# A gated FNet layer in split float32: y's sums placed behind the operands, part two's rows and first tokens loaded a chunk sooner, y's last copies set between the pairs of weights

## The chip, the core and the metric

One core of a Trainium2 chip runs the whole program. Its engines work at the same time, each through its own list in order: TensorE (PE) multiplies, VectorE (DVE) and ScalarE (ACT) work on elements, SyncE (SP) issues most of the DMAs, and GpSimd (POOL) does next to nothing here. An instruction waits for the results it needs, and everything behind it in the same list waits with it. The metric is the time of one execution on the device in microseconds (us).

## What is computed

S = 2048 tokens, D = 512, F = 1792, all float32:

```python
xn = layernorm(x)                                   # rows of 512
a, b = xn @ dft_hid_re.T, xn @ dft_hid_im.T
y = dft_seq_re @ a - dft_seq_im @ b                 # FNet mixing, 2048 x 512
h = relu(xn @ w1 + b1) ** 2
out = x + y * silu(h @ w2 + b2)
```

The kernel transforms along the sequence first and along the hidden dimension second; the sum is the same.

## The kernel before

**Arithmetic.** Every float32 operand is split into a high part (ACT, `split_hi`, line 77) and a low part (DVE, `split_lo`, line 80), and a product is three matmuls: high by high, high by low, low by high. Large products use a scheme of seven block products in place of eight. It needs sums of blocks of the operands, made by DVE ahead of the split (`sums_b`, lines 212 to 214: one row of 512 elements, two of 256), and sums of the seven results (`combine`, lines 255 to 265).

**Part one, first transform.** The sequence transform goes in eight chunks `c` of 256 frequencies; each goes through eight steps `j` over the tokens. Chunks 0 and 1 are plain products. Chunks 2 to 7 use the seven products: 42 matmuls in step (c, j), called group (c, j) here, line 453, on the PSUM banks m_bb, m_b and m_ba. The operand of a step is a tile of the transform's matrix: loaded by SP into `r` (two buffers, so a load waits until the split of two steps earlier has read it), summed into `t` (`prep_sums`), split into `g` (`prep_parts`). It is made two steps ahead of its use.

**Part one, second transform.** The result of chunk c - 1 (tile `plain` or `c` in the profile) is transformed along the hidden dimension while chunk c runs, again as seven products of 12 matmuls each, one per step (line 428, `y<-...`). In order of time they take the operands A11, S2, S3, A22, A12, S1, S4. `y_make(b, i)` makes operand number i: a split (`y_A`, `y_S`), and at some steps a sum of blocks (`y_sum`, line 385). `y_product` multiplies, `y_result` copies a product out or adds it (line 442, `ysb<-y,ysb`). The sixth product, S1's, begins in the same PSUM tile that the fifth one's add reads, so PE waits there for that add. Three of the seven need a sum of blocks of the hidden transform's matrix (`yw`, tiles `y_t`). `y_sums`, advanced step by step by `next(t3)`, makes these sums once, during chunk 2: it loads blocks (`y_t<-in_wd`), adds (lines 349, 353, 359, 366), splits (lines 339/340 or 77/80), and stores them to DRAM (`td`). The later chunks load them back (`y_load`, line 328), in the same two buffers.

**Weights of part two.** While chunks 3 to 6 run, `make_w` makes the sums and splits of one piece of w1 per chunk and stores it (`jobs`, `w0hi`, `w1d`).

**Part two** goes through 28 hidden units (four chunks of 512 tokens by seven pieces of F), 42 matmuls each (line 779, `hps`), on two sets of PSUM banks by turns: even units on b2, ba and bb, odd ones on b3 and bc. ACT copies a unit's first product out (line 784), DVE combines it (lines 256 to 265), ACT squares it, and it is stored (`hd`). A unit can begin only when the unit two before it is combined. Its tokens are loaded raw (`in_xt`), normalised by DVE with `rows`, the means and factors of LayerNorm (line 479, two instructions), summed and split into `xT` (`xt_half`, a generator of four steps). The tokens of the first 512 are made in chunk 7 (tile `stage`), each half in four calls of `next(staged[q])`. After the hidden units come the products with w2 (line 833).

**The passage between the parts.** y of the last chunk is not done in seven products: after the first hidden unit, `stage2` multiplies it as two plain products (line 307, `yps`), in banks bc and ba, and ACT copies each out (line 313, `ysb<-yps`). Beside it the last pieces of w1 (5 and 6, `v5`, `v6`) and two pieces of w2 (2 and 3, `w2`, `w3`; tiles `w2raw`, `w2g0a`, `w2g1a`) are loaded, summed, split and, for w2, stored; `go("w2", ...)` takes one step of each name. Both w2 pieces use the same raw buffer.

The order on every engine is that of the program: nothing is moved by a scheduler.

Of the kernel before, what the change touches and what calls it, by code (L numbers as in the profile page):

```python
# [11 lines left out]
ALU = mybir.AluOpType  # L12

P = 128
# [4 lines left out]
NC = S // CW  # L19
# [22 lines left out]
S1 = A21  # L42
# [28 lines left out]
def fnet_gated_kernel(ctx, tc, x, xt, ct, wd, w1, w2, b1, b2, out):  # L71
# [31 lines left out]
    def buf(tag, shape, name, dtype=F32, bufs=1):  # L103
        return pool.tile(shape, dtype, tag=tag, bufs=bufs, name=name)

    def bcast(src, n):
        return bass.AP(tensor=src.tensor, offset=src.offset, ap=[[0, P], [1, n]])
# [218 lines left out]
    def y_load(n):  # L326
        for q, t in enumerate(y_matrix(n)):
            nc.sync.dma_start(t.bitcast(F32), TD[n][q])
# [54 lines left out]
    def y_sum(b, to, x_, y_, op, place):  # L383
        v = y2[b]
        nc.vector.tensor_tensor(v[place], v[x_], v[y_], op=op)
        v[to] = v[place]

    def y_make(b, i):

        if i == 0:  # L390
            y_part(b, "A11", 0)
            y_sum(b, "S1", "A21", "A22", ALU.add, "A21")
        elif i == 1:
            y_sum(b, "S2", "S1", "A11", ALU.subtract, "A11")
            y_part(b, "S2", 1)
        elif i == 2:
            y_part(b, "A22", 0)

            y_sum(b, "S3", "A22", "S2", ALU.subtract, "A22")
        elif i == 3:  # L400
            y_part(b, "S3", 1)
            y_sum(b, "S4", "A12", "S2", ALU.subtract, "A11")
        elif i == 4:
            y_part(b, "A12", 1)
        elif i == 5:
            y_part(b, "S1", 0)
        elif i == 6:
            y_part(b, "S4", 1)
# [51 lines left out]
    def load_rows(c, t):  # L460

        flat = rows.rearrange("a b -> (a b)")
        for m in range(2):
            for h in range(2):
                n = m * S + c * TC + h * 256
                nc.sync.dma_start(t[:, 2 * m + 1 - h], bcast(flat[n:n + 256], 256))
        xT["rows"] = t
# [49 lines left out]
    def stores():  # L517
        while later:
            later.pop(0)()
# [44 lines left out]
    def prep_sums(between=None):  # L564
        if todo:
            s = todo[0]
            making_[s] = moving(f"{s[0]}_{s[1]}", raw[s], between)
            next(making_[s])
# [121 lines left out]
    last_plain((2, 0), (3, 0))  # L690
    split_s1(NJ - 1)
    prep(close_plain)
    next(t3)
    y_begin(1, copy.rearrange("p k (m t n) -> p k m t n", m=2, t=2)[:, :, ::-1], (0, 1, 2, 3))


# [186 lines left out]
        nc.vector.tensor_tensor(z, z, fin[c][2 + k // 2][:, k % 2, w], op=ALU.add)  # L883
        nc.sync.dma_start(at(out[c * TC:(c + 1) * TC], k)[:, cols], z.rearrange("p (k e) -> p k e", e=256))

    jobs, staged, w1_late = {}, {}, {}
    for c, j in steps:
        last = c == NC - 1
        if j == 0:
            ms = banks(c)  # L890
        g = part.pop((c, j))
        for p in ORDER:
            a, (grp, b) = PRODUCTS[p]
            mm(product(ms, p), XC[j][:, a], lambda b_: g[grp][:, b_, b], j == 0, j == NJ - 1)

        i = j - 2 + last
        done = (c - 2, 6) if j == 0 and c > PLAIN else (c - 1, i) if 0 <= i < 7 else None
        stores()
        prep_sums()

        y_make(c - 1, i + 1)
        if c == PLAIN and j in (0, 1, 4, 5, 6, 7):
            next(t3)
        if c in JOBS and j < 6:
            if j == 0:
                jobs[c] = make_w(*work.pop(0), *(buf(f"pq1{k}", [P, 4, 256], f"w{c}_{k}") for k in range(2)))
            next(jobs[c])
        if last:
            for q, js in ((0, (3, 4, 5)), (1, (4, 5, 6))):
                if j in js:  # L910
                    next(staged[q])
        if done:
            y_product(*done)
        if j == NJ - 1:
            e = buf("e", [P, 4, 512], f"c{c}")
            combine(e, ms)
            rows_ = y_result(*done)
            if not last:

                y_begin(c, e.rearrange("p (m i) (d t n) -> p (i d) m t n", m=2, d=2, t=2), (2, 3, 0, 1))  # L920
        prep_parts()
        if done:
            if j < NJ - 1:
                rows_ = y_result(*done)
            later.extend(lambda v=v: y_put(*v) for v in rows_)
        if c > PLAIN and i in (-1, 1, 3):
            y_load({-1: 2, 1: 4, 3: 1}[i])
        if c == PLAIN and j == 4:
            nc.vector.transpose(stats_t, stats.rearrange("p m h j -> p (m h j)"))
            for q in range(4):  # L930
                nc.sync.dma_start(rows[:, q * 32:(q + 1) * 32], stats_t[q * 32:(q + 1) * 32, :])
        if last:

            if j in (2, 3):
                q = j - 2
                t = buf(f"xc{2 + q}", [P, 3, 4, 256], f"stage{q}")
                if q == 0:
                    load_rows(0, t[:, 0])
                    b2s = buf("st", [P, D], "b2s")
                    nc.sync.dma_start(b2s, bcast(b2, D))  # L940
                staged[q] = xt_half(0, q, lambda k, t=t: t[:, 1 if k == "r" else 2])
                next(staged[q])
            if j == 4:
                nc.sync.dma_start(WD[0][:, :, :, CW:].bitcast(F32), B12D)
            if j > 3:
                load_w1(j - 4)
            if j == 6:
                w1_late[5] = late_w1(5)
                next(w1_late[5])
# [10 lines left out]
    def go(*names):  # L960


        for v in names:
            k, n = v[0], int(v[1:])
            if k == "m":
                load_rows(n, buf("pq00", [P, 4, 256], f"rows{n}"))
            elif k == "l":
                load_w2(n)
            elif k != "h" or n < len(units):
                if v not in making:  # L970
                    making[v] = {"h": lambda: operand(n, *units[n]), "x": lambda: tokens(n // 2, n % 2),
                                 "w": lambda: late_w2(n), "v": lambda: late_w1(n)}[k]()
                next(making[v])
# [38 lines left out]
    for n, (c, p) in enumerate(units):  # L1012
        ahead, behind = beside.get((c, p), ((), ()))
        go(*ahead)
        unit = hidden(n, c, p)
        next(unit)
        if n == len(units) - 1:

            m26, m4 = bank("b2", "m_b2_o0"), bank("ba", "m_ba_o0")
            bias(m26[:, 0], 2)  # L1020
            bias(m4[:, 0], 4)
        if before:
            next(before)
        next(unit)
        if n == 0:

            making["v5"] = w1_late[5]
            load_w1(4)
            go("w2", "v5", "v5", "v6", "w2", "w2", "w2", "w3", "v6", "v6", "w3", "w3", "w3")
            stage2(NC - 1, 0)  # L1030
            stage2(NC - 1, 1, "ba")
        go(*behind)
        before = unit
    m1, m7, m53 = bank("bb", "m_bb_o0"), bank("bc", "m_bc_o0"), bank("b3", "m_b3_o0")
    bias(m53[:, 0], 5)
# [147 lines left out]
```

## Time and profile before

| | |
|---|---|
| median of 3 runs | 752.03 us (749.72 to 752.36) |
| the profiled execution | 752.59 us, of which the span is 750.8 us |
| mean granted clock of TensorE in it | 0.973 |
| moved by DMA | 157.91 MB, mean 210 GB/s |

The profile is of one execution. Durations and waits below come from it; "idle before" is the time an engine stood ahead of an instruction, with the engine or DMA that ended the wait. The granted clock is that of the throttle on TensorE: 1.00 in most stretches of 10 us, 0.72 between 160 and 170 us, and 0.59 between 460 and 470 us.

### The profile page before, as it was taken

What the parts mean: (1) busy time and instruction counts of PE and PEld (TensorE: products, weight loads), DVE (VectorE), ACT (ScalarE), POOL (GpSimd) and SP (SyncE); (2) the same over time, 40 slices, a digit from 0 to 9 for tenths busy, and PEclk for the clock granted to TensorE, in tenths of its full rate; (3) what the DMA queues carried; (4) which work ended last, traced back from release to release, by engine and by line L of the source; (5) the groups of instructions that cost most, each with busy time, mean ns of one, the idle gap of its engine ahead of it and who ended that gap; (6) DMA issues with size and microseconds to landing.
All of it is one profiled execution on the core that took longest, in us unless ns stands there. A gap on an engine that the chain in (4) does not pass through costs nothing.

```text
span 750.8 us, 13275 instructions
## 1 busy us (share of the span) xinstructions
PE 712.7 (95%) x5368; PEld 682.8 (91%) x5368; DVE 634.9 (85%) x939; ACT 361.2 (48%) x498; POOL 5.2 (1%) x8
## 2 busy tenths in 40 slices
PE   8999998989999999999997794999999999999996
PEld 5778788989999999999997783999999999999996
DVE  7999758979988889898884874699998889989897
ACT  4435543532634535426432324476767774535441
POOL 0000000000000000000000000000000000101000
PEclk9999999989999999999998896999999999999999
DMA  8443664264746745647455976365562796676844
GB/s 306 143 164 112 213 228 167 87 224 168 253 146 232 253 152 198 242 153 258 138 191 194 419 290 251 141 252 211 214 249 105 291 379 267 196 229 159 248 132 155
DMA packets 61821, 157.91 MB, mean 210 GB/s; under 512 B 5824, under 2 KB 26560, under 8 KB 60608
## 3 DMA queue, kind: packets, MB, share of 16 engines
q1 hardware_dynamic: 53760, 136.75, 52.7%
q10 hardware_dynamic: 6912, 19.27, 6.7%
q0 software_dynamic: 1088, 1.05, 1.0%
q8 instruction: 42, 0.69, 0.3%
q14 instruction: 19, 0.16, 0.1%
HBM read 113.25 MB, written 43.79 MB: 209 GB/s over the span
## 4 chain that ended last, share of the span: by engine, by line
PE 62%; DVE 22%; DMA 7%; issue 4%; ACT 4%; SPq 1%; ACTq 0%; DVEq 0%
PE m_b_o L833 9%; PE hps L779 9%; PE m_b L453 8%; PE pq_b L551 7%; DVE g L80 6%; PE hps_b L779 4%; PE y L428 4%; PE m L833 3%; DVE t L212 2%; PE hps_ba L779 2%; DMA w2raw<-in_w 2%; PE m_bb_o L833 2%; DMA stage<-in_xt 2%; PE m_bb L453 2%; PE yps L307 1%
## 5 line engine op out<-in xcount | busy, mean ns | idle before, releaser
L453 PE MATMUL m_b<-g,xc 128*128 128x256 f32 x1440 | 184.3, 286 | 0.0
L453 PEld LDWEIGHTS m_b<-g,xc 128*128 128x128 f32 x1440 | 180.1, 195 | 0.1
L77 ACT ACTIVATE g<-r 128x768 fp32r<-128x768 f32 (+2 forms) x65 | 57.6, 886 | 76.0 <-PE m_b L453 60.9
L779 PE MATMUL hps<-xT,w 128*128 128x256 f32 x504 | 66.0, 292 | 13.2 <-ACT ysb L313 11.0
L779 PEld LDWEIGHTS hps<-xT,w 128*128 128x128 f32 x504 | 64.6, 201 | 13.8 <-ACT ysb L313 11.4
L80 DVE TENSOR_TENSOR g<-r,g 128x768 fp32r<-128x768 f32 (+2 forms) x65 | 65.4, 1006 | 13.3 <-ACT g L77 13.1
L833 PE MATMUL m_b_o<-w,g 128*128 128x256 f32 x588 | 75.3, 282 | 0.0
L833 PEld LDWEIGHTS m_b_o<-w,g 128*128 128x128 f32 x588 | 72.3, 191 | 0.1
L551 PE MATMUL pq_b<-g,xc 128*128 128x512 f32 x240 | 67.0, 397 | 1.5 <-ACT xc L77 1.4
L80 DVE TENSOR_TENSOR g<-t,g 128x1024 fp32r<-128x1024 f32 x48 | 58.6, 1220 | 5.4 <-ACT g L77 5.4
L77 ACT ACTIVATE g<-t 128x1024 fp32r<-128x1024 f32 x48 | 50.4, 1050 | 25.6 <-DVE t L214 19.3
L551 PEld LDWEIGHTS pq_b<-g,xc 128*128 128x128 f32 x240 | 43.7, 187 | 14.8 <-ACT xc L77 3.6
L453 PE MATMUL m_bb<-g,xc 128*128 128x256 f32 x288 | 44.6, 291 | 8.2 <-DVE g L80 6.1
L453 PEld LDWEIGHTS m_bb<-g,xc 128*128 128x128 f32 x288 | 39.4, 197 | 9.2 <-DVE g L80 6.5
L790 ACT ACTIVATE h<-h,b1s 128x512 f32<-128x512 f32 x56 | 37.4, 715 | 18.7 <-DVE h L264 18.7
L77 ACT ACTIVATE g<-hr 128x768 fp32r<-128x768 f32 (+1 forms) x28 | 35.5, 1267 | 21.1 <-DVE hr L220 7.8
L80 DVE TENSOR_TENSOR g<-hr,g 128x768 fp32r<-128x768 f32 (+1 forms) x28 | 41.6, 1485 | 2.3 <-ACT g L77 2.2
L453 PE MATMUL m_ba<-g,xc 128*128 128x256 f32 x288 | 42.0, 281 | 0.0
L453 PEld LDWEIGHTS m_ba<-g,xc 128*128 128x128 f32 x288 | 37.7, 189 | 0.0
L779 PE MATMUL hps_b<-xT,w 128*128 128x256 f32 x288 | 36.2, 281 | 0.0
L779 PEld LDWEIGHTS hps_b<-xT,w 128*128 128x128 f32 x288 | 35.1, 190 | 0.0
L212 DVE TENSOR_TENSOR t<-r 128x512 f32<-128x512 f32 x48 | 33.1, 689 | 1.2
(210 smaller groups left out, 1189.4 us busy)
## 6 DMA issues: line engine op xcount, KB each, us to landing
r<-in_ct SPq DMA_DIRECT2D x63, 512.0 KB, 4.0
y_t<-td SPq DMA_DIRECT2D x30, 512.0 KB, 5.7
hd<-h ACTq DMA_DIRECT2D x28, 512.0 KB, 3.8
hr<-hd SPq DMA_DIRECT2D x28, 512.0 KB, 3.9
w<-w1d SPq DMA_DIRECT2D x5, 1792.0 KB, 11.4
w<-w2d SPq DMA_DIRECT2D x4, 1792.0 KB, 10.4
y<-ysb SPq DMA_DIRECT2D x16, 256.0 KB, 4.2
w2d<-w2g1a SPq DMA_DIRECT2D x4, 1024.0 KB, 6.5
```

The source lines that it names most:

```text
L77: nc.scalar.activation(hi, src, AF.Copy)
L80: return nc.vector.tensor_tensor(lo, src, hi.bitcast(F32), op=ALU.subtract)
L212: nc.vector.tensor_tensor(t[:, 0:2], r[:, 0:1].to_broadcast([P, 2, 256]), r[:, 1:3], op=ALU.add)
L307: ins = nc.tensor.matmul(ps, PQ[c, m, k // 2][:, a_, w:w + P], WD[m, k][:, b_, :], start=n == 0, stop=n == 2 * ND * 3 - 1)
L428: nc.tensor.matmul(ps, g[:, a_, q], m, start=n in (1, 2, 5) and q == 0 and (a_, b_) == (HI, HI), stop=q == ND - 1 and (a_, b_) == (LO, HI) ...
L453: ins = nc.tensor.matmul(ps[:, d * CW:(d + 1) * CW], w[:, a_, d * P:(d + 1) * P], mv(b_), start=first and d == 0 and (a_, b_) == (HI, HI), ...
L551: ins = nc.tensor.matmul(accs[c][k], w, part[c, j][:, b_, 2 * h:2 * h + 2], start=j == 0 and h == 0 and (a_, b_) == (HI, HI), stop=j == NJ ...
L779: nc.tensor.matmul(product(ms, k), W1[p][a][:, a_, q * P:(q + 1) * P], xT[c, q][:, b_, b], start=share not in first, stop=q == 1 and (a_, ...
L790: nc.scalar.activation(x_[:, s], x_[:, s], AF.Relu, bias=b1s[:, f:f + 1])
L833: nc.tensor.matmul(m[:, k * 256:(k + 1) * 256], g[:, a_, a, k * P:(k + 1) * P], W2[p][:, b_, b], start=p == 0 and k == 0 and (a_, b_) == ( ...
```

## The change

- Chunk 2: the steps of `y_sums` come at the end of a step, behind `prep_parts`, in each of the first seven steps; before, one stood ahead of the loop and six stood between `prep_sums` and `prep_parts` of steps 0, 1, 4, 5, 6 and 7.
- `y_make`: the sum S2 is made one step sooner, with S1's. In the step that uses S3 (`i == 2`), S3's operand is made ahead of `prep_sums`; in the others behind it, as before.
- The jobs of `make_w` run in steps 0 and 2 to 6 instead of 0 to 5, so all but their first move one step back.
- `rows` and the first half's raw tokens are loaded at the end of chunk 6, in the buffers pq10 and pq11; the two tiles `stage` in xc2 and xc3 become one in xc2, loaded in step 2 of chunk 7 with the second half's tokens. The other steps of `staged` are spread over steps 1, 3, 4, 5 and 6.
- In the passage, the first copy of `stage2` stands behind w2's split of piece 2, the second behind v6, and the sums, splits and stores of piece 3 come after `go(*behind)`, which loads the rows and tokens of the next 512.

```diff
@@ y_make
         if i == 0:
             y_part(b, "A11", 0)
             y_sum(b, "S1", "A21", "A22", ALU.add, "A21")
+            y_sum(b, "S2", "S1", "A11", ALU.subtract, "A11")
         elif i == 1:
-            y_sum(b, "S2", "S1", "A11", ALU.subtract, "A11")
             y_part(b, "S2", 1)
@@ ahead of chunk 2
     prep(close_plain)
-    next(t3)
     y_begin(1, copy.rearrange("p k (m t n) -> p k m t n", m=2, t=2)[:, :, ::-1], (0, 1, 2, 3))
@@ the loop over (c, j), chunks 2 to 7
         stores()
+
+        if i == 2:
+            y_make(c - 1, i + 1)
         prep_sums()
-
-        y_make(c - 1, i + 1)
-        if c == PLAIN and j in (0, 1, 4, 5, 6, 7):
-            next(t3)
-        if c in JOBS and j < 6:
+        if i != 2:
+            y_make(c - 1, i + 1)
+        if c in JOBS and j in (0, 2, 3, 4, 5, 6):
...
         if last:
-            for q, js in ((0, (3, 4, 5)), (1, (4, 5, 6))):
-                if j in js:
-                    next(staged[q])
+            for q in {1: (0,), 3: (0,), 4: (1,), 5: (0,), 6: (1, 1)}.get(j, ()):
+                next(staged[q])
...
         if c > PLAIN and i in (-1, 1, 3):
             y_load({-1: 2, 1: 4, 3: 1}[i])
+        if c == PLAIN and j < 7:
+            next(t3)
...
+        if c == NC - 2 and j == NJ - 1:
+            load_rows(0, buf("pq10", [P, 4, 256], "rows0"))
+            staged[0] = xt_half(0, 0, lambda k: buf("pq11", [P, 4, 256], "xr0_0") if k == "r" else stage[0][:, 0])
+            next(staged[0])
         if last:
-
-            if j in (2, 3):
-                q = j - 2
-                t = buf(f"xc{2 + q}", [P, 3, 4, 256], f"stage{q}")
-                if q == 0:
-                    load_rows(0, t[:, 0])
-                    b2s = buf("st", [P, D], "b2s")
-                    nc.sync.dma_start(b2s, bcast(b2, D))
-                staged[q] = xt_half(0, q, lambda k, t=t: t[:, 1 if k == "r" else 2])
-                next(staged[q])
+            if j == 2:
+
+                stage.append(buf("xc2", [P, 3, 4, 256], "stage"))
+                staged[1] = xt_half(0, 1, lambda k: stage[0][:, 1 if k == "r" else 2])
+                next(staged[1])
+                b2s = buf("st", [P, D], "b2s")
+                nc.sync.dma_start(b2s, bcast(b2, D))
@@ the passage, n == 0
-            go("w2", "v5", "v5", "v6", "w2", "w2", "w2", "w3", "v6", "v6", "w3", "w3", "w3")
+            go("w2", "v5", "v5", "v6", "w2", "w2")
             stage2(NC - 1, 0)
+            go("w2", "w3", "v6", "v6")
             stage2(NC - 1, 1, "ba")
         go(*behind)
+        if n == 0:
+            go("w3", "w3", "w3")
```

PE's list holds the same instructions in the same order. Three places where the other lists change:

DVE in chunk 2, around S3's operand (`y_S<-plain`); t_6 and g_2_6 belong to group (2,6), `y_t` in lines 359 and 340 is the second stored sum of y's matrix. Before:

```order
L80 TENSOR_TENSOR g_2_5_1244<-t_5_1221,g_2_5_1244 128x1024
L212 TENSOR_TENSOR t_6_1292<-r_6_1175 128x512
L213 TENSOR_TENSOR t_6_1292<-t_6_1292,r_6_1175 128x256
L214 TENSOR_TENSOR t_6_1292<-t_6_1292,r_6_1175 128x256
L80 TENSOR_TENSOR y_S_1296<-plain,y_S_1296 128x512
L385 TENSOR_TENSOR plain<-plain 128x4x128
L359 TENSOR_TENSOR y_t_905<-y_t_905,y_t_906 128x1024
L340 SCALAR_TENSOR_TENSOR y_t_1_1302<-y_t_905,y_t_0_1301 128x1024
L80 TENSOR_TENSOR g_2_6_1317<-r_6_1175,g_2_6_1317 128x768
```

And of the change:

```order
L80 TENSOR_TENSOR g_2_5_1244<-t_5_1221,g_2_5_1244 128x1024
L359 TENSOR_TENSOR y_t_905<-y_t_905,y_t_906 128x1024
L340 SCALAR_TENSOR_TENSOR y_t_1_1252<-y_t_905,y_t_0_1251 128x1024
L80 TENSOR_TENSOR y_S_1297<-plain,y_S_1297 128x512
L385 TENSOR_TENSOR plain<-plain 128x4x128
L212 TENSOR_TENSOR t_6_1301<-r_6_1172 128x512
L213 TENSOR_TENSOR t_6_1301<-t_6_1301,r_6_1172 128x256
L214 TENSOR_TENSOR t_6_1301<-t_6_1301,r_6_1172 128x256
L80 TENSOR_TENSOR g_2_6_1317<-r_6_1172,g_2_6_1317 128x768
```

The three sums of t_6 went from ahead of S3's split to behind it, and the sum of y's matrix with its split from behind to ahead.

SP from the end of chunk 6 to the middle of chunk 7; `rows` and `in_xt` are what part two's tokens need, y_t the matrices of y, r the operands' raw tiles. Before, the loads stand in the middle of chunk 7:

```order
L201 DMA r_6_4180<-in_ct 128x1024
L328 DMA y_t_0_4183<-td_84 128x1024
L328 DMA y_t_1_4184<-td_84 128x1024
L466 DMA stage_4187<-rows 128x256 x4
L940 DMA b2s<-in_b 128x512
L473 DMA stage_4187<-in_xt 128x1024
L201 DMA r_7_4265<-in_ct 128x1024
L473 DMA stage_4268<-in_xt 128x1024
```

And of the change, from the end of chunk 6 on:

```order
L201 DMA r_3_3956<-in_ct 128x1024
L466 DMA rows_3958<-rows 128x256 x4
L473 DMA xr_0_3963<-in_xt 128x1024
L447 DMA y_70<-ysb_3570 128x512
L201 DMA r_4_4039<-in_ct 128x1024
L328 DMA y_t_0_4042<-td_83 128x1024
L328 DMA y_t_1_4043<-td_83 128x1024
```

Rows and the first tokens stand behind r_3 instead of behind r_6, with a put of y, r_4 and y's matrix behind them.

ACT in the passage; w2raw, w2g0a and w2g1a are a piece of w2, w1raw, w1a and w1b the last piece of w1, `h_1<-hps_1` the copy of unit 1's first product. Before:

```order
L77 ACTIVATE w2g1a_4644<-w2raw_4625 128x1024
L77 ACTIVATE w1a_4655<-w1raw_4636 128x768
L77 ACTIVATE w1b_4656<-w1sums_4651 128x1024
L77 ACTIVATE w2g0a_4664<-w2raw_4649 128x768
L77 ACTIVATE w2g1a_4667<-w2raw_4649 128x1024
L313 ACTIVATE ysb_4697<-yps_0_4672 128x512
L313 ACTIVATE ysb_4697<-yps_1_4700 128x512
L784 ACTIVATE h_1_4780<-hps_1_4737 128x256
```

And of the change:

```order
L77 ACTIVATE w2g1a_4645<-w2raw_4626 128x1024
L313 ACTIVATE ysb_4673<-yps_0_4648 128x512
L77 ACTIVATE w1a_4684<-w1raw_4637 128x768
L77 ACTIVATE w1b_4685<-w1sums_4680 128x1024
L313 ACTIVATE ysb_4673<-yps_1_4690 128x512
L77 ACTIVATE w2g0a_4729<-w2raw_4678 128x768
L77 ACTIVATE w2g1a_4732<-w2raw_4678 128x1024
L783 ACTIVATE h_1_4781<-hps_1_4738 128x256
```

The two copies of y went from behind both pieces of w2 to behind the first piece and behind w1's last piece; the copy of unit 1's first product stands behind the second piece of w2, as before.

2 lines of the change are left out of this document (1 added, 1 removed).

## The prediction

> **What bounds the kernel now.** I read the page's busy times first, then the waits of TensorE (PE), then the timeline around each wait.
>
> ```profile
> PE 712.7 (95%) x5368; PEld 682.8 (91%) x5368; DVE 634.9 (85%) x939; ACT 361.2 (48%) x498; POOL 5.2 (1%) x8
> PE hps L779 <- ACT ysb L313: 11.0, 1, 11.0
> PE m_bb L453 <- DVE g L80: 6.1, 2, 5.1
> PE y L428 <- issue: 4.0, 1, 4.0
> PE y L428 <- DVE ysb L442: 2.4, 1, 2.4
> PE hps L779 <- DVE h L265: 2.2, 1, 2.2
> PE y L428 <- DVE y_S L80: 1.9, 4, 0.7
> PE m_bb L453 <- ACT g L77: 1.6, 1, 1.6
> ```
>
> PE is busy for 95% of the span, and its order is the same in both kernels. So time can only come from PE's waits and from what follows a wait: a stretch of slower matmuls. Columns of the timeline: start, duration, engine, line, count, and in brackets the idle time ahead with its releaser.
>
> ```profile
> 130.46 0.88 PE L453 MATMUL m_bb<-g,xc 128*128 128x256 f32 x6
> 134.73 0.88 PE L453 MATMUL m_ba<-g,xc 128*128 128x256 f32 x6
> 163.58 2.15 PE L428 MATMUL y<-y_t,y_S 128*128 128x256 f32 x12 [2.38 <-DVE ysb L442]
> 166.29 1.65 PE L453 MATMUL m_bb<-g,xc 128*128 128x256 f32 x6 [0.57 <-ACT c L255]
> 172.91 0.88 PE L453 MATMUL m_ba<-g,xc 128*128 128x256 f32 x6
> ```
>
> The first 36 matmuls of a group take 4.27 us from start to start at full clock (134.73 - 130.46), but 6.62 us (172.91 - 166.29) behind the wait of 2.38 us: 2.35 us are lost to the clock there. Every wait below is priced with this tail.
>
> **Chunk 2: sums of y's matrix behind the operands.** The same DVE instructions stand between group (2,1)'s operands and the add L442 on which PE waits at 163.58; only their order changes. So L442 can gain no more than DVE's idle time there.
>
> ```profile
> 140.89 0.68 DVE L80 TENSOR_TENSOR y_S<-plain,y_S 128x512 fp32r<-128x512 f32 x1
> 141.84 1.58 PE L428 MATMUL y<-wd,y_S 128*128 128x256 f32 x12
> 142.10 1.22 DVE L359 TENSOR_TENSOR y_t<-y_t,y_t 128x1024 f32<-128x1024 f32 x1
> 145.58 0.95 DVE L80 TENSOR_TENSOR g<-r,g 128x768 fp32r<-128x768 f32 x1
> 157.46 1.23 DVE L366 TENSOR_TENSOR y_t<-y_t,y_t 128x1024 f32<-128x1024 f32 x1 [3.30 <-DMA y_t<-in_wd]
> 163.02 0.41 DVE L442 TENSOR_TENSOR ysb<-y,ysb 128x256 f32<-128x256 f32 x1
> ```
>
> The two waits at 121 to 122.6 (1.6 and 1.0 us) go, since the sums no longer stand ahead of group (2,2)'s operands. What is late next is S3's operand: the sum L359 with its split (142.10 to 145.58, 3.48 us) now stands ahead of y_S instead of behind it, while the t sums go behind. PE, 2.6 us and a tail earlier, then waits some 5 us (the wait moved in, 3.5, and what DVE is behind anyway) at the product that ran without a wait at 141.84. That is a moved wait, not an added one: DVE sets the end. Of the idle 3.30 us most stays, because the last two loads of wd now leave SP behind r_0, which waits for group (2,6)'s split. The load that L359 needs leaves behind r_6, too, and may come some 0.6 us late (it is issued about 5 us ahead of its use). L442 lands between 159.7 (163.02 - 3.30) and 163.6. I take 162.5, near the present row. Chunk 3's first group follows it by 3.27 us as now (166.29 - 163.02), at 165.8: 0.5 us gained, and 2.35 more because PE should come to L442 with next to no wait and then run at full clock. **Term 1: 2.8 us**, from -0.6 (later by 0.6, tail kept) to 5.6 (3.3 + 2.35).
>
> **S3 first, chunks 3 to 6.**
>
> ```profile
> L212 DVE TENSOR_TENSOR t<-r 128x512 f32<-128x512 f32 x48 | 33.1, 689 | 1.2
> ```
>
> In each, PE waits once for y_S: the row with 1.9 us in four times. S3's split now stands ahead of the next group's three t sums; the first of them alone takes 689 ns, as long as the longest wait (0.7 us), and two shorter ones follow. **Term 2: 1.9 us** (0 if DVE runs later by that much, else 1.9). S2's sum, a step sooner, only takes away DVE's wait for ACT ahead of S2's split. The weight job moved one step back costs nothing: it lies in the same DVE and ACT slack, and its stores are read only in part two; without that cover one of its splits, about as long as a t sum (0.7 us), would come back as a wait.
>
> **Chunk 7: rows and first tokens a chunk sooner.**
>
> ```profile
> 364.31 10.53 SPq L201 DMA_DIRECT2D r<-in_ct  x2
> 383.68 0.69 DVE L80 TENSOR_TENSOR y_S<-c,y_S 128x512 fp32r<-128x512 f32 x1 [0.76 <-ACT y_S L77]
> 392.92 2.02 SPq L466 DMA_DIRECT2D stage<-rows  x4
> 405.01 2.48 DVE L479 TENSOR_TENSOR stage<-stage 128x1024 f32<-128x1024 f32 x2 [9.46 <-DMA stage<-in_xt]
> 408.42 1.44 PE L453 MATMUL m_bb<-g,xc 128*128 128x256 f32 x5 [5.05 <-DVE g L80]
> 414.99 0.88 PE L453 MATMUL m_ba<-g,xc 128*128 128x256 f32 x6
> 426.23 2.03 PE L428 MATMUL y<-y_t,y_S 128*128 128x256 f32 x12 [3.96 <-issue]
> 433.48 0.88 PE L453 MATMUL m_ba<-g,xc 128*128 128x256 f32 x6
> ```
>
> DVE stood 9.46 us for the tokens; PE lost 5.05 us, then 2.4 to the clock (6.57 against 35/36 of 4.27), and at 426.23 another 3.96 us (DVE's lateness again: L442 stands behind the staged work) with 1.6 behind it (433.48 - 426.23 = 7.25, against 12/36 of 4.27 and 4.27). Together 13.0 us. Now rows and tokens leave SP behind r_3, at about 375 (the second r of the row at 364.31). From the first row load to the use of the tokens it took 12.1 us (405.01 - 392.92), which gives 387. DVE reaches the new place, behind S2's y_S at about 383.5, and waits up to 3.5 us; through L479 (2.5) and group (7,3)'s operands this comes to at most 1.8 us at S3's product, nothing if the tokens take 8 us. I take 1.0. What waits on SP behind these five issues is y's put, r_4 and y's matrix; r_4 is used some 10 us later, which hides it. The second half has its rows by then and needs only the tokens. The other staged work is the same work in gaps that DVE had as idle time. **Term 3: 12.0 us**, from 9 (the W1 loads, packed closer, delay y's matrix) to 13.0.
>
> **Part two: y's last copies between the weights.** The chain of waits tells this stretch (start, us, what).
>
> ```profile
> 439.72 9.01 DMA w2raw<-in_w
> 453.39 6.28 DMA w2raw<-in_w
> 462.35 0.59 ACT ysb L313
> 462.98 6.57 PE hps L779 x34
> 469.55 7.46 DMA xr<-in_xt
> 477.04 1.24 DVE xr L479
> 485.90 0.70 DVE h L256
> 488.63 6.04 PE hps L779 x36
> ```
>
> ```profile
> 440.64 11.36 PE L307 MATMUL yps<-wd,pq 128*128 128x512 f32 x48
> 450.39 1.06 ACT L77 ACTIVATE w2g1a<-w2raw 128x1024 fp32r<-128x1024 f32 x1 [0.80 <-DVE w2raw L214]
> 462.48 1.23 DVE L80 TENSOR_TENSOR w2g1a<-w2raw,w2g1a 128x1024 fp32r<-128x1024 f32 x1 [0.30 <-ACT w2g1a L77]
> 499.49 5.12 PE L779 MATMUL hps<-xT,w 128*128 128x256 f32 x42
> ```
>
> Unit 1 needs the bank of y's first copy. The matmuls end at 452.0 (440.64 + 11.36); the copy now stands behind the first w2g1a (ends 451.45) and is done at 452.05. So unit 1 starts at 452.1 and not at 462.98. The late wait comes next: on ACT the copy of unit 1's first bank stands behind the second w2raw, and PE needs it for unit 3. That load leaves 0.3 us later (one more put on SP), lands at 460.0, and its sums and splits end 4.0 us on (463.71 - 459.67, by the row of w2g1a and the load), at 464.0; a combination takes 2.7 until PE goes on (485.90 to 488.63), to 466.7. PE is at unit 3 by 462.2 (two units of about 5.0, 42/36 of 4.27): it waits some 3.7 us, six matmuls already issued taken off. The tokens, which now leave behind the second copy instead of behind both w2 stores, land before 467. From there DVE is the bound: from L479 to the next combination 8.9 us (477.04 to 485.90), and 2.7 for that one, hence 478.4 for unit 5, whose part behind L265 started at 488.63. From there to unit 7 it took 10.9 us (499.49 - 488.63). On PE alone it would be 9.3 (36 matmuls and a unit); DVE works in that stretch too and needs between that and 10.9. I take 10.9, the row: unit 7 starts at 489.3 and not at 499.49. **Term 4: 10.2 us**; up to 11.8 if only PE bounds (487.7), down to 6 if the second w2raw lands 2.7 us later (9.0 as the first load did, not 6.3) and the first one 1.5 later.
>
> **A rule weighed.** By "TensorE: Matmul & The Clock Gate" of the Trainium skill, section "Why this matters for your kernels", only idle gaps over about 3 us drop the clock. The row at 163.58 speaks against it: 2.38 us of idle were enough for slow matmuls. By that rule the tails behind 163.58 and 488.63 would have another cause and would stay; that case is the second rival.
>
> **Sum.** 2.8 + 1.9 + 12.0 + 10.2 = 26.9 us. The profiled execution took 752.59 us (its span of 750.8 and 1.8 around it), which gives 725.7; the median of the runs, 752.03, lies 0.6 lower. I forecast **726**. Low ends together (-0.6 + 0 + 9 + 6 = 14.4) give 738, high ends (5.6 + 1.9 + 13.0 + 11.8 = 32.3) give 720.
>
> **Rivals.**
> - The loads crowd. Chunk 7 is shorter by some 10 us, yet carries the same W1 loads; w2raw's first load took 9.01 us beside two of them. Each us that it or the next w2raw lands later is a us at unit 1 or 3. With 5 there in all, and 2 in chunk 7: 733. For it: that load's 9 us against the second one's 6.28; against it: only two W1 loads stand right ahead of it, as before.
> - The slow tails do not come from the waits. Then 2.35 us (chunk 2) and 1.6 us (unit 5: 6.04 us against some 4.4) stay: 726 + 3.9 = 730. Against it: no slow stretch in the timeline stands without idle time ahead.
> - Chunk 2 does not do what it says: the wait moves to S3 and a tail reaches the end of the chunk. Without term 1: 728.5.
> - Slower than before: SP holds the second w2raw. A put of y, which waits for ACT, now stands ahead of it; ACT waits for the first w2raw; and the copy that frees unit 3's bank stands behind the second one. Each us that this load lands later is a us for PE. From 27 us later than 460 on, the total is above the present one; 35 us later gives 726 + 35 = 761. For it: SP issues in order, and here it stood for DVE's splits. Against it: the two loads of this tile landed 6.3 and 9 us after their issue, and ACT has nothing left to wait for once w2g1a is done (451.45).
> - No change: DVE, busy 85%, bounds more than I see, and each wait comes back elsewhere: about 751. Against it: DVE's idle 9.46 and 3.30 us stand at just these places.
>
> **Chances.** Forecast (722 to 730): 0.60; crowded loads (730 to 737) 0.16; tails elsewhere 0.07; chunk 2 nothing 0.05; better than all terms (under 720) 0.05; no change 0.04; slower 0.03. A measurement of this kernel tells about 0.5% (3.8 us) from no change. Faster 0.93, within 0.04, slower 0.03. The range 719 to 737 leaves out 0.12 at most.
>
> **What would show it.** In the changed profile: no PE wait on ysb L313 and unit 1 within 1 us of y's last matmul; a new wait of 3 to 4 us at unit 3 (hps behind DVE's L265 or ACT's copy); no wait over 1 us in chunks 3 to 6; in chunk 2 a wait of some 5 us on y_S; DVE's wait for the staged tokens under 4 us. I am wrong if the second w2raw lands past 465, if SP stands behind the rows for long, or if PE's tails show without waits.

## The result, and the profile after

| | before | after |
|---|---|---|
| median of the runs | 752.19 us (4 runs) | 733.0 us (4 runs, 731.84 to 734.61) |
| ratio | | 0.9752, 95% interval 0.9722 to 0.9781 |
| the profiled execution; its span | 752.59 us; 750.8 us | 733.17 us; 731.4 us |
| mean granted clock of TensorE | 0.973 | 0.987 |

The kernel is 19.4 us faster between the two profiled executions; 26.9 had been forecast (726 us). PE's busy row, and all waits of PE over 1 us but that of its warm-up, after:

```profile
PE 706.9 (97%) x5368; PEld 677.2 (93%) x5368; DVE 634.2 (87%) x939; ACT 360.5 (49%) x498; POOL 5.2 (1%) x8
PE y L428 <- ACT y_S L77: 4.8, 1, 4.8
PE y L428 <- ACT ysb L440: 3.2, 2, 1.7
PE hps L778 <- ACT ysb L313: 2.9, 1, 2.9
PE hps L778 <- DVE h L265: 2.1, 1, 2.1
...
PE y L428 <- DVE ysb L442: 1.2, 1, 1.2
PE m_bb L453 <- ACT c L255: 1.1, 1, 1.1
PE m_b L453 <- DVE c L264: 1.0, 1, 1.0
```

The waits of 5.1 us (the tokens) and 4.0 (L442 in chunk 7) are gone, and so are the four at y_S in chunks 3 to 6; that of 11.0 (y's copy) is down to 2.9. Of the new ones, the longest stands in chunk 2, at S3's product; the two at L440 are one of 1.65 in chunk 2 and one of 1.58 in chunk 7. A wait of 2.1 for L265 stands in part two, as one of 2.2 did before. PE does the same list in both kernels, so its instructions cut the time into stages that can be compared, each by the start of its first matmul:

| us | before | after | gained | forecast |
|---|---|---|---|---|
| start to group (3,1) (chunk 2 and the first group of chunk 3) | 175.03 | 178.13 | -3.1 | 2.8 |
| (3,1) to (7,0) | 195.74 | 192.67 | 3.1 | 1.9 |
| (7,0) to y's plain products (`yps`) | 69.87 | 58.05 | 11.8 | 12.0 |
| `yps` to unit 7 | 58.85 | 51.06 | 7.8 | 10.2 |

The four sum to 19.6; the 0.2 us less in the spans (750.8 - 731.4 = 19.4) lies behind unit 7. Two terms came as forecast or better, one is 2.4 us short, and the first one has the wrong sign. Its stage in the changed kernel, from the timelines of PE, DVE, ACT and SP:

```profile
133.76 1.38 SPq L336 DMA_DIRECT2D y_t<-in_wd  x1
140.85 1.23 DVE L359 TENSOR_TENSOR y_t<-y_t,y_t 128x1024 f32<-128x1024 f32 x1 [2.38 <-DMA y_t<-in_wd]
143.79 0.80 PE L428 MATMUL y<-wd,y_S 128*128 128x256 f32 x2 [4.76 <-ACT y_S L77]
145.13 2.50 PE L428 MATMUL y<-wd,y_S 128*128 128x256 f32 x10 [0.55 <-DVE y_S L80]
152.53 0.84 ACT L77 ACTIVATE g<-r 128x768 fp32r<-128x768 f32 x1 [3.36 <-PE m_b L453]
153.40 0.96 DVE L80 TENSOR_TENSOR g<-r,g 128x768 fp32r<-128x768 f32 x1 [1.53 <-ACT g L77]
158.98 1.23 DVE L366 TENSOR_TENSOR y_t<-y_t,y_t 128x1024 f32<-128x1024 f32 x1 [3.40 <-DMA y_t<-in_wd]
166.60 0.42 DVE L442 TENSOR_TENSOR ysb<-y,ysb 128x256 f32<-128x256 f32 x1
169.89 0.97 PE L453 MATMUL m_bb<-g,xc 128*128 128x256 f32 x6 [1.06 <-ACT c L255]
173.83 2.36 PE L453 MATMUL m_b<-g,xc 128*128 128x256 f32 x18 [1.00 <-DVE c L264]
```

Read it in order. The block that L359 adds leaves SP at 133.76, behind a load of `r` that stood there until its buffer was free, and two stores; DVE stands 2.38 us for it. Before, this load had left at 123.93 and nobody waited. S3's operand is behind that sum, so PE waits 4.76 and 0.55 us, and the ten matmuls that follow are slow (2.50 us). PE is then late in releasing a buffer of `g`, ACT waits 3.36 us for it ahead of a split of `g`, and DVE 1.53 us for ACT. The wait of 3.30 at L366 is still there, as 3.40. DVE's two new waits (2.38 + 1.53 = 3.9), less 0.3 from smaller ones that came or went (0.70 at S2's split among them), are L442's delay: 163.02 before, 166.60 now.

Part two, after:

```profile
427.93 0.33 SPq L735 DMA_DIRECT2D w2raw<-in_w  x1
428.85 11.36 PE L307 MATMUL yps<-wd,pq 128*128 128x512 f32 x48
439.90 0.69 DVE L212 TENSOR_TENSOR w2raw<-w2raw 128x512 f32<-128x512 f32 x1 [4.31 <-DMA w2raw<-in_w]
442.51 0.58 ACT L313 ACTIVATE ysb<-yps 128x512 f32<-128x512 f32 x1
443.14 7.97 PE L778 MATMUL hps<-xT,w 128*128 128x256 f32 x42 [2.93 <-ACT ysb L313]
452.32 0.69 DVE L212 TENSOR_TENSOR w2raw<-w2raw 128x512 f32<-128x512 f32 x1 [4.58 <-DMA w2raw<-in_w]
458.98 6.04 PE L778 MATMUL hps<-xT,w 128*128 128x256 f32 x36 [2.12 <-DVE h L265]
479.91 5.12 PE L778 MATMUL hps<-xT,w 128*128 128x256 f32 x42
```

y's matmuls end at 440.21, but its copy stands on ACT behind the first w2raw's split, and that load, issued at 427.93, was there only at 439.9: 11.97 us (9.01 before).

### The profile page after: what moved, and what is told of

It is laid out like the page before. It is cut to its first block, busy times and chain, and to the rows that moved or that the text cites. A ratio compares the mean times of both kernels' runs of the same rounds, so it can differ in the third digit from the quotient of the medians.

```text
span 731.4 us, 13281 instructions
## 1 busy us (share of the span) xinstructions
PE 706.9 (97%) x5368; PEld 677.2 (93%) x5368; DVE 634.2 (87%) x939; ACT 360.5 (49%) x498; POOL 5.2 (1%) x8
## 4 chain that ended last, share of the span: by engine, by line
PE 80%; DVE 9%; DMA 7%; issue 2%; ACT 2%; SPq 1%; DVEq 0%; ACTq 0%
PE m_b L453 17%; PE m_b_o L832 10%; PE hps L778 9%; PE pq_b L551 7%; PE y L428 6%; PE hps_b L778 5%; PE m_bb L453 4%; PE m_ba L453 3%; PE m L832 3%; DMA w2raw<-in_w 3%; DMA y_t<-in_wd 3%; PE hps_ba L778 2%; PE m_bb_o L832 2%; DVE g L80 2%; PE yps L307 2%
## 5 line engine op out<-in xcount | busy, mean ns | idle before, releaser
L453 PE MATMUL m_b<-g,xc 128*128 128x256 f32 x1440 | 179.1, 281 | 1.3 <-DVE c L264 1.0
L453 PEld LDWEIGHTS m_b<-g,xc 128*128 128x128 f32 x1440 | 174.4, 189 | 1.7 <-issue 1.2
L453 PE MATMUL m_bb<-g,xc 128*128 128x256 f32 x288 | 42.7, 285 | 1.1 <-ACT c L255 1.1
## 6 DMA issues: line engine op xcount, KB each, us to landing
w<-w2d SPq DMA_DIRECT2D x4, 1792.0 KB, 10.2
```

The costliest lines, as they stand in the source:

```text
L453: ins = nc.tensor.matmul(ps[:, d * CW:(d + 1) * CW], w[:, a_, d * P:(d + 1) * P], mv(b_), start=first and d == 0 and (a_, b_) == (HI, HI), ...
```

## Experiments

Each kernel is the changed one with one edit, or with several where the heading says so. The table has every run by the stages above; the last stage goes to unit 8, since in one of the runs unit 7 itself was broken up by waits. Ratios are to the kernel before, with their 95% intervals.

| run | L442 | to (3,1) | (3,1) to (7,0) | (7,0) to yps | yps to unit 8 | median | ratio |
|---|---|---|---|---|---|---|---|
| before | 163.02 | 175.03 | 195.74 | 69.87 | 63.80 | 752.19 | |
| after | 166.60 | 178.13 | 192.67 | 58.05 | 56.02 | 733.0 | 0.9752 (0.9722 to 0.9781) |
| e1 | 162.87 | 174.42 | 192.67 | 57.58 | 55.50 | 729.21 | 0.9712 (0.9686 to 0.9739) |
| e2 | 160.58 | 172.13 | 192.67 | 57.61 | 56.73 | 727.37 | 0.9673 (0.9648 to 0.9698) |
| e3 | 164.62 | 176.17 | 192.67 | 57.91 | 55.71 | 732.16 | 0.9740 (0.9714 to 0.9766) |
| e4 | 166.65 | 178.19 | 192.68 | 57.81 | 52.90 | 730.58 | 0.9722 (0.9697 to 0.9747) |
| e5 | 159.18 | 170.71 | 192.68 | 57.76 | 55.58 | 725.05 | 0.9653 (0.9628 to 0.9678) |
| e6 | 166.66 | 178.21 | 192.67 | 57.55 | 57.80 | 735.5 | 0.9787 (0.9758 to 0.9816) |
| e7 | 159.24 | 170.79 | 192.67 | 59.79 | 56.87 | 727.8 | 0.9682 (0.9657 to 0.9707) |
| e8 | 166.57 | 178.09 | 192.67 | 58.76 | 56.84 | 733.97 | 0.9765 (0.9740 to 0.9791) |
| e9 | 168.44 | 179.99 | 192.67 | 57.94 | 55.28 | 733.56 | 0.9763 (0.9737 to 0.9789) |
| e10 | 168.43 | 179.95 | 192.67 | 57.88 | 58.49 | 737.46 | 0.9809 (0.9780 to 0.9838) |
| e11 | 159.49 | 171.04 | 192.67 | 59.89 | 58.15 | 729.8 | 0.9707 (0.9681 to 0.9733) |
| e12 | 159.32 | 170.87 | 192.67 | 58.22 | 52.17 | 722.69 | 0.9599 (0.9585 to 0.9613) |

A stage that an edit doesn't touch shows what one execution can differ by: `yps` to unit 8 is 55.3 to 56.8 in after, e1, e2, e3, e5, e8 and e9, and chunk 2 of the unedited order ends 1.8 us later in e10 than in e4 (its load for L359 landed later, and DVE waited 3.56 us).

### e1: chunk 2's sums put back

```diff
     prep(close_plain)
+    next(t3)
...
+        if c == PLAIN and j in (0, 1, 4, 5, 6, 7):
+            next(t3)
...
-        if c == PLAIN and j < 7:
-            next(t3)
```

> The changed kernel, with the five sums of y's matrix in chunk 2 put back to where they stood before (ahead of the operands); everything else of the change stays. Theory A (in chunk 2 the sums behind the operands cost time, since their loads from wd leave SP late and DVE idles for them): L442 at the end of chunk 2 comes back from 166.60 to 163.0 give or take 0.4, chunk 3's second group (3,1) from 178.1 to about 175.0, and the time falls from 733.0 by about 3 us, to 730. Rival (what is lost in chunk 2 comes from another part, such as S2 or S3 computed sooner): L442 stays at 166 or later and the time at 733.

L442 at 162.87 and group (3,1) at 174.42, 3.7 us sooner than after; 729.21 us. With the rest of the change in place, this part of it costs 3 to 4 us.

### e2: the loads from wd ahead of those of r

```diff
-        prep_parts()
+        s_ = todo[0] if todo else None
+        prep_parts(not (c == PLAIN and j < 7))
...
         if c == PLAIN and j < 7:
             next(t3)
+            load_more(s_)
```

`load_more` is the loop over `load_c` that stood at the end of `prep_parts`.

> The changed kernel, with chunk 2's loads of raw operands (r) issued on SP behind the step of the sums in each step of the loop, so that the loads from wd for L359 and L366 leave before them. Theory A (the late loads are the cause): the load for L359 leaves at 130 to 131 rather than 133.76, DVE's waits of 2.38 at L359 and 3.40 at L366 go, L442 comes at 160.8 to 162.5 rather than 166.60, and the time is 727 to 729. Theory B (the place of S3's operand behind L359's sum is the cause, by PE's wait of 4.76): S3's operand still stands behind the sum, PE still waits 2 us or more for it at clock under 0.8, L442 gains under 2.5 us, and the time is 731 to 733.

From the timelines of SP, PE and DVE:

```profile
129.91 0.55 SPq L336 DMA_DIRECT2D y_t<-in_wd  x1
141.41 0.50 PE L428 MATMUL y<-wd,y_S 128*128 128x256 f32 x2 [2.29 <-ACT y_S L77]
142.75 1.63 PE L428 MATMUL y<-wd,y_S 128*128 128x256 f32 x10 [0.84 <-DVE y_S L80]
150.87 0.96 DVE L80 TENSOR_TENSOR g<-r,g 128x768 fp32r<-128x768 f32 x1 [1.37 <-ACT g L77]
160.58 0.42 DVE L442 TENSOR_TENSOR ysb<-y,ysb 128x256 f32<-128x256 f32 x1
```

The load leaves 3.85 us sooner, neither L359 nor L366 waits any more, and L442 comes 6.0 us sooner: theory A. It even beats the order of before, since the 3.30 us at L366, which the change had left standing, go too. PE still waits 2.29 and 0.84 us for S3's operand, and DVE still gets 1.37 us of that back.

### e3: S3's operand ahead of L359's sum

```diff
-        if i == 2:
+        if i == 2 and c > PLAIN:
             y_make(c - 1, i + 1)
...
+        if c == PLAIN and j == 3:
+            y_make(c - 1, 3)
         if c == PLAIN and j < 7:
             next(t3)
```

> The changed kernel, with S3's operand (and the sum S4) in chunk 2 made a step sooner, ahead of L359's sum; the loads from wd leave as in the changed kernel. Theory A (the late loads set it, and DVE the end): PE's wait of 4.76 at S3's product goes, but DVE still idles 1 us or more at L359 and about 3 at L366; L442 gains 1.3 us or so and the time is 731.5 to 733. Theory B (S3's place): with PE's wait of 4.76 its slow stretch and DVE's wait of 1.53 for PE's release go too, L442 gains 3 to 5 us, and the time is 728 to 730.

```profile
139.03 1.66 PE L428 MATMUL y<-wd,y_S 128*128 128x256 f32 x12
140.91 1.23 DVE L359 TENSOR_TENSOR y_t<-y_t,y_t 128x1024 f32<-128x1024 f32 x1 [1.11 <-DMA y_t<-in_wd]
156.95 1.23 DVE L366 TENSOR_TENSOR y_t<-y_t,y_t 128x1024 f32<-128x1024 f32 x1 [4.26 <-DMA y_t<-in_wd]
```

PE runs through S3's product, and L442 comes only 1.98 us sooner: DVE's 1.53 for PE's release is gone and its wait at L359 is 1.27 shorter, but the one at L366 is 0.86 longer. PE's longest wait of the stage was not its price. Theory A again.

### e5: both

The diffs of e2 and e3 together.

> The changed kernel, with both edits of chunk 2: the raw operands' loads behind the sums' step on SP, and S3's operand ahead of L359's sum. Theory A (DVE sets the end of chunk 2, by its work and what idle time is left): the wait of 2.29 and 0.84 on PE at S3's product and DVE's 1.37 for PE's release, which the first edit alone left, go as well; L442 at 158.5 to 160 (160.58 with the first edit alone, 164.62 with the second alone), and the time is 725 to 727. Rival (with the loads early the place of S3 no longer matters, since PE's wait lies beside DVE's work): L442 at 160.3 or later and the time at 727.4.

L442 at 159.18, 725.05 us: theory A. With the loads early, S3's place is worth another 1.4 us, through the wait for PE's release, which is gone from DVE's rows.

### e8, e9 and a probe in e12: what took away the waits in chunks 3 to 6

Three parts of the change touch these chunks: S3's operand first, S2's sum a step sooner, and the weight job shifted by a step. e8 undoes the first, e9 the first two.

```diff
# e8 and e9
-        if i == 2:
-            y_make(c - 1, i + 1)
         prep_sums()
-        if i != 2:
-            y_make(c - 1, i + 1)
+        y_make(c - 1, i + 1)
# e9 also
-            y_sum(b, "S2", "S1", "A11", ALU.subtract, "A11")
         elif i == 1:
+            y_sum(b, "S2", "S1", "A11", ALU.subtract, "A11")
```

> The changed kernel, with S3's operand back behind the sums of the next operand in every chunk (term 2 of the prediction undone, everything else as changed). Theory (each wait for S3's operand costs its length and some 0.25 us more in the matmuls that restart behind it): the waits of 0.2 to 0.75 at chunks 3 to 6 come back, from group (3,1) to (7,0) PE takes about 195.7 rather than 192.67, and the time is 736. Rival (the waits cost only their length): 194.6 and 735. Rival two (they cost nothing, since chunk 7 absorbs them): 733, with yps at 428.9 as in the changed kernel.

> The changed kernel, with S3's operand back behind the next operand's sums (as in the run before that undid it alone, and gave back no wait) and the sum S2 back one step later; of the change in chunks 3 to 6 only the weight job's shift by a step is left. Theory (S2 computed a step sooner is what took the four waits away): from group (3,1) to (7,0) PE takes 195 to 196 again rather than 192.67, with one wait for y_S in each chunk, and the time is 735 to 737. Rival (the weight job's shift took them away): 192.7, and 733 to 734.

Both take 192.67 us from (3,1) to (7,0), as after: no wait came back, and the theories of both runs fell; the rival named for e9, the weight job's shift, held. That shift is enough by itself. DVE's rows of chunk 5 before show how, at the step that makes S2:

```profile
286.79 0.68 DVE L385 TENSOR_TENSOR c<-c 128x512 f32<-128x512 f32 x1
288.18 0.69 DVE L80 TENSOR_TENSOR y_S<-c,y_S 128x512 fp32r<-128x512 f32 x1 [0.70 <-ACT y_S L77]
288.79 0.68 DVE L80 TENSOR_TENSOR w<-w,w0hi 128x512 f32<-128x512 f32 x1
290.00 0.96 DVE L80 TENSOR_TENSOR g<-r,g 128x768 fp32r<-128x768 f32 x1 [0.53 <-ACT g L77]
```

DVE stands 0.70 us for ACT's half of the split, and 0.53 us more because ACT has the job's split (`w0hi`) ahead of `g`'s. S3's split comes two steps later and is late by about this much. The job's shift puts its DVE sums there in place of a split: in e9 the 0.70 at S2 is still there and the 0.53 is gone. S2 sooner takes the 0.70 away. The last run has the job of chunk 5 alone at its old steps, with S2 and S3 as changed:

```diff
-        if c in JOBS and j in (0, 2, 3, 4, 5, 6):
+        if c in JOBS and j in (range(6) if c == 5 else (0, 2, 3, 4, 5, 6)):
```

There chunk 5's groups still follow each other by 6.40 us (PE, groups (5,4), (5,5) and (5,6)):

```profile
288.19 0.87 PE L453 MATMUL m_bb<-g,xc 128*128 128x256 f32 x6
294.58 0.88 PE L453 MATMUL m_bb<-g,xc 128*128 128x256 f32 x6
300.98 0.87 PE L453 MATMUL m_bb<-g,xc 128*128 128x256 f32 x6
```

So either edit does it alone: the job's shift (e9, in all four chunks), or S2 and S3 sooner (the probe, in chunk 5, whose wait was the longest). Undoing one part shows nothing where another covers for it.

### e4: the first w2raw ahead of a W1 load

```diff
+            go("w2")
             load_w1(4)
-            go("w2", "v5", "v5", "v6", "w2", "w2")
+            go("v5", "v5", "v6", "w2", "w2")
```

> The changed kernel, with part two's first load of raw w2 issued on SP ahead of load_w1(4) (1792 KB) rather than behind it; buffers set its issue at 427.9 in both. Theory (the W1 load issued 2 us ahead holds up w2raw's landing, and that is what is left of term 4): w2raw lands 7 to 9 us after its issue rather than 11.97, PE's wait of 2.93 at unit 1 shrinks to under 0.5, the second w2raw leaves and lands 3 us or more sooner and the wait of 2.12 at unit 3 shrinks; the time falls by 3 to 6 us, to 727 to 730. Rival (the order on the queue doesn't decide: all transfers under way share the engines, or the copies of y wait for something else): w2raw still takes 11 us or more, the waits stay, 733.

```profile
427.76 0.33 SPq L735 DMA_DIRECT2D w2raw<-in_w  x1
435.04 0.85 ACT L77 ACTIVATE w2g0a<-w2raw 128x768 fp32r<-128x768 f32 x1 [0.88 <-DMA w2raw<-in_w]
437.94 0.58 ACT L313 ACTIVATE ysb<-yps 128x512 f32<-128x512 f32 x1
439.88 5.20 PE L778 MATMUL hps<-xT,w 128*128 128x256 f32 x42
451.50 0.97 PE L778 MATMUL hps<-xT,w 128*128 128x256 f32 x6 [1.38 <-ACT h L783]
455.09 6.64 PE L778 MATMUL hps<-xT,w 128*128 128x256 f32 x36 [2.62 <-DVE h L265]
```

ACT begins on w2raw 7.3 us after its issue, and unit 1 follows y's matmuls without a wait, as forecast for the change. The wait at unit 3 stays (1.38 and 2.62), against my expectation, since DVE begins on the second w2raw 3.9 us sooner but PE is ready for unit 3 some 6 us sooner. The stage is 3.1 us shorter; the runs show 2.4, where 3 to 6 had been expected.

### e6 and e10: the second piece of w2 moved out of the way

e6 moves its sums, split and store behind unit 1's combination, e10 its load too.

```diff
# with e4's edit; e6
-        if n == 0:
+        if n == 1:
             go("w3", "w3", "w3")
# e10
-            go("w2", "w3", "v6", "v6")
+            go("w2", "v6", "v6")
...
-        if n == 0:
-            go("w3", "w3", "w3")
+        if n == 2:
+            go("w3")
+        if n == 3:
+            go("w3", "w3", "w3")
```

> The changed kernel, with part two's first w2raw ahead of load_w1(4) on SP, and the sums, split and store of the second raw w2 moved from behind unit 0 to behind unit 1's combination (its load stays where it is). Theory (unit 3 waits 2.62 for unit 1's combination, which stands on DVE and ACT behind the second w2raw): PE's waits of 1.38 and 2.62 at unit 3 go with their slow matmuls (6.64 for 36 where 42 take 5.20 elsewhere), unit 7 begins at 471 to 473.5 rather than 476.63, and the time is 725.5 to 728. Rival (the work only moves: units 4 or 5 then wait for it): unit 7 at 475 or later, 729 to 731.

> The changed kernel, with the first w2raw ahead of load_w1(4), and the whole of the second raw w2's work (load, sums, split, store) moved behind units 2 and 3. Theory (the run that moved only its sums lost 7.43 us of DVE to the tokens of the next part, which landed at 454.97 behind the second w2raw; PE is bound there by what the queue has to bring before them): rows and tokens leave SP about 4 us sooner and land by 451, units 3 and 4 wait less than 1 us each, unit 7 begins at 471 to 474 (479.91 as changed, 476.63 with the first w2raw first), and the time is 726 to 728.5. Rival (the tokens' landing is set by the W1 load and the stores, not by the second w2raw): tokens at 453 or later, a wait of 3 us or more at unit 3 or 4, unit 7 at 477 or later, 731 or more.

Both are slower than e4, by 5 and 7 us, and e6 is slower than either of its expectations. e6, rows of SP, DVE and PE:

```profile
446.90 1.64 SPq L473 DMA_DIRECT2D xr<-in_xt  x2
449.71 5.20 PE L778 MATMUL hps<-xT,w 128*128 128x256 f32 x42
454.97 2.48 DVE L479 TENSOR_TENSOR xr<-xr,rows 128x1024 f32<-128x1024 f32 x2 [7.43 <-DMA xr<-in_xt]
457.38 0.68 DVE L212 TENSOR_TENSOR w2raw<-w2raw 128x512 f32<-128x512 f32 x1
460.39 1.65 PE L778 MATMUL hps_bb<-xT,w 128*128 128x256 f32 x6 [5.48 <-ACT h L783]
```

Unit 3 (449.71) has no wait left, and unit 4 has one of 5.48. The tokens of the next part, 8.1 us after their issue, are what DVE stands for now: 7.43 us, with nothing to do. In the changed kernel and in e4 it has the second w2raw's sums and splits in that gap; moved behind it, they come on top, ahead of unit 2's combination. In e10 the tokens leave ahead of the second w2raw, yet arrive at 455.83, 7.6 us after their issue at 448.23. Moving that load behind them did not bring them sooner, as the rival there said; what sets their 8 us is not shown. 1.8 of e10's 7 us are chunk 2's, as told under the table.

### e7, e11, e12: the parts together

e7 is e5 with e6's edits, e11 is e5 with e10's, e12 is e5 with e4's and the probe.

> The changed kernel with the two edits of chunk 2 and the two of part two together. If the two places are independent, their gains add up: about 7 us of chunk 2 and 5 to 7 of part two, 719 to 722. If an earlier end of chunk 7 makes part two's loads denser, so that w2raw lands late again, 723 or more.

> The two edits of chunk 2 (wd loads ahead, S3's operand ahead) with the two of part two of the run before this one. If the gains add up, 725.05 less 5 to 7 us: 718 to 721. If part two's edits fail or its loads bind again with chunk 7 ending 7.7 us sooner, 724 or more.

> The two edits of chunk 2 with the first w2raw ahead of load_w1(4) and nothing else in part two; and in chunk 5 alone the weight job at its old steps (0 to 5), as a probe. Time: 725.05 less the 2.4 that the w2raw edit gave alone, 722 to 723.5, if the two places add up; 724.5 or more if the W1 loads bind again. Probe: theory (the job's shift is what took the waits away, whatever stands ahead of S3) says that chunk 5's fourth group takes 7.2 to 7.4 us to the fifth again, with a wait of 0.5 to 0.8 for y_S, where chunks 3, 4 and 6 take 6.40; rival (S3 ahead of the next operand's sums, with S2 a step sooner, is enough by itself: either of the two edits removes the waits) says 6.40 in chunk 5 too.

The gains of the two places add up: e12 is 2.4 us below e5, as e4 is below the changed kernel. At 722.69 us (0.9599, interval 0.9585 to 0.9613) it is the fastest version of this study, 10 us below the changed kernel. e7 and e11 inherit the losses of e6 and e10, and their chunk 7 took 2 us more than that of e5: the wait for the copy of y, which stands there in all runs with the change (1.06 to 2.26 us), was 1.79 and 1.97 in these two, with slow matmuls behind it. In e12 it was 1.75 and in e8 2.26, at full pace.

## Why the prediction was right, and where it was off

The measured 733.0 us lies inside the forecast range of 719 to 737, but not in the narrower 722 to 730 that had been given 0.60. It lies in the part given to the crowded loads (0.16), and that is partly luck: of what fell short, these are some 2.4 us, and 5.9 are chunk 2, whose -3.1 us lies below its own lowest value of -0.6.

**Term 1, chunk 2: +2.8 forecast, -3.1 measured.** This is the step that failed. Its frame held: DVE sets the end of the chunk, S3's operand becomes late, PE waits some 5 us there (4.76 + 0.55), and the 3.30 us at L366 stay. Three steps in it were wrong.
- "The load that L359 needs ... may come some 0.6 us late (it is issued about 5 us ahead of its use)". It was issued 4.7 us ahead of the point where DVE was ready (138.47) and took 7.1: DVE lost 2.38 us. Before, the same load took 7.0 us, but with a lead of 18. e2 shows that this is the cause, and that the queue behind `r` is what made it late.
- "A moved wait, not an added one". PE's wait at S3 was priced at nothing because DVE sets the end. But DVE itself waits for buffers that PE reads, and PE's lateness came back as 1.53 us. e5 against e2 shows it: with DVE's 1.37 for PE's release gone, L442 comes 1.40 sooner. In e3 the 1.53 goes too, and waits for the loads change beside it.
- The slow tail of 2.35 us in chunk 3's first group did go (0.97 us for the first six matmuls, 1.65 before), but the group took only 0.5 us less (8.24, 8.74 before). At full clock PE reaches the banks before DVE has combined them: it waits 0.29 and 1.00 us for `combine` inside the group, and 1.06 (0.57 before) ahead of it.

With L442 3.58 us later and 0.5 us back, the sum is -3.1.

**Term 2, chunks 3 to 6: +1.9 forecast, +3.1 measured.** The waits went, but the reason was half of it. I had given the gain to S3's place and nothing to the weight job's shift; e9 shows that the shift alone removes all four, and the probe that S2 and S3 sooner remove the longest without it. The size was low by a quarter of a us for each wait, with the matmuls that start again: before, the group with the 0.49 us wait took 7.15 us and its neighbours 6.40.

**Term 3, chunk 7: +12.0 forecast, +11.8 measured.** It went as the steps said: DVE waited 0.83 us for the tokens (3.5 had been the bound); the row names no releaser, but their load landed at 384.44. The 1.0 us set aside for S3's product came elsewhere, as 1.58 us at the product before it, S2's: ACT's copy of the first product waits until the put of the previous block's y has read its buffer.

```profile
382.42 0.32 SPq L447 DMA_DIRECT2D y<-ysb  x1
384.52 2.49 DVE L479 TENSOR_TENSOR xr<-xr,rows 128x1024 f32<-128x1024 f32 x2 [0.83 <-issue]
389.88 0.38 ACT L440 ACTIVATE ysb<-y 128x256 f32<-128x256 f32 x1 [5.62 <-DMA y<-ysb]
390.32 1.68 PE L428 MATMUL y<-y_t,y_S 128*128 128x256 f32 x12 [1.58 <-ACT ysb L440]
```

That put left SP at 382.42 among the loads which the change moved there, and ACT went on 7.5 us later. Before, it left at 380.83, ACT went on 7.5 us later too, and PE lost 0.2 us. Two things stand in the 1.6 us between: the add that the put stores begins 0.8 later, with S2's sum now ahead of it (381.15, 380.38 before), and SP then waits 0.6 for one of the moved loads of `rows`. An order that puts it ahead of them, or a second buffer, was not tried.

**Term 4, part two: +10.2 forecast, +7.8 measured.** The mechanism held: y's copies no longer wait for the second piece of w2, and unit 3 waits for it instead (2.12 us; 3.7 forecast). The copy itself came 2.9 us late, since the first w2raw took 11.97 us where the row of before, 9.01, had been used. This is the rival "the loads crowd", at 2.4 us rather than its 5 and 2. Two W1 loads (1792 KB each) stood ahead of w2raw, 5.3 and 2.0 us sooner, in both kernels, as the forecast had noted; but they took 7.6 and 9.8 us before and 11.2 and 12.7 after, where the same loads fall in a chunk 7 that is 11.8 us shorter. e4 shows that the W1 load counts: with one of the two behind w2raw instead of ahead of it, ACT starts on it 7.3 us after its issue and unit 1 has no wait. That the shorter chunk is what made the loads slower fits the rival, but no run tests it. The slower rival, SP standing long ahead of the second w2raw, did not come: that load left at 444.84 and was used from 452.32. Nothing was seen of "no change". Against the rival by which the slow tails do not come from the waits: the tails behind the waits of 2.38 and 3.96 went with the waits, and e4 has no slow matmul at unit 1 once the wait there is gone. Of the signs named in advance, one failed (unit 1 was to follow y's last matmul within 1 us, without a wait for L313), one failed barely (1.06 us in chunk 3, where no wait over 1 was to be) and one was weaker (2.12 us at unit 3, not 3 to 4); the wait of some 5 us at y_S in chunk 2 and the short wait for the tokens came.

All together: -5.9 (term 1), +1.2 (term 2), -0.2 (term 3) and -2.4 (term 4) against the forecast are -7.3, and 725.7 + 7.3 is 733.0, within 0.2 us of the profiled run. It is terms 1 and 4: in both a load landed later than I had taken from a single row, and in term 1 PE's lateness came back as well, and waits for `combine` took most of the tail that was to be gained.

## What to carry to other kernels

When work is moved behind something on a compute engine, look at what its loads are then queued behind: here a load of 0.5 MB that had 18 us of lead (123.93 to 142.10) kept 5, and landed in 7. A wait beside the engine that sets the end is not free if that engine needs buffers which the waiting one releases. And an idle gap that has to be waited out anyway is the best place for work: taking the work out of it only adds the work's length later.

## What the runs showed of the hardware that I had not expected

**The slow matmuls behind a wait.** PE's rows show waits after which the matmuls run at full pace, and others of the same length after which they don't (where PE doesn't wait, 12 take 1.60 us and 42 take 5.20, which makes 4.46 for 36):

| wait, us | run and start | matmuls behind it |
|---|---|---|
| 1.83 | e3, 147.50 | 12 in 1.70: full pace |
| 1.79 | e7, 383.19 | 12 in 2.58: slow |
| 2.26 | e8, 390.96 | 12 in 1.70: full pace |
| 2.56 | e10, 467.43 | 36 in 4.54: full pace |
| 2.62 | e5, 435.14 | 42 in 5.30: full pace |
| 2.62 | e4, 455.09 | 36 in 6.64: slow |
| 2.44 | e2, 436.21 | 42 in 6.78: slow |
| 2.93 | after, 443.14 | 42 in 7.97: slow |
| 3.65 | e1, 163.44 | 12 in 2.90: slow |

The clock's rows go with it: the granted clock was 0.66 between 440 and 450 us after, where the wait of 2.93 stands. From chunk 2 on, single waits up to 1.75 us were harmless, those from 2.9 on were not, and between them it went both ways, so a tail behind such a wait (1.0 to 2.8 us in the slow rows here) is a chance and not a sum. Two shorter waits close together were not harmless: before, PE waited 1.59 us at 121.17 and 1.01 at 122.57, and the 30 matmuls from 123.26 on took 5.24 us, where 3.72 is full pace. The Trainium skill, page "TensorE: Matmul & The Clock Gate", section "Why this matters for your kernels", asks for no idle gaps above about 3 us to keep the clock up. These runs agree above that, but show slow stretches behind single waits from 1.79 us on.

**How long a load takes.** The same 512 KB of w2raw took 9.0, 12.0 and 7.3 us in before, after and e4: with two W1 loads close ahead of it in the first two, which themselves took longer after, and with one in e4.
